# Zero matmuls ahead of the prologue, and traced costs for a planner's exponentials and score matmuls

## The chip, the cores and the metric

The kernel runs on one core of a Trainium2 chip. The metric is the device time of one execution in microseconds (us). Before the change the median of three runs is 796.83 us (796.32 to 798.67). One more execution was taken with the hardware profiler; its records are the profile and the trace read below. Five engines work at the same time, each through its own list of instructions in order: TensorE (PE, matmuls; its weight loads are shown as PEld), VectorE (DVE), ScalarE (ACT), GpSimd (POOL) and SyncE (SP), which only issues transfers here.

## The reference

Two branches are added to the input, for one sequence of 2,048 rows of 512 numbers in bf16.

```python
def _A_ref(x, wqkv, wo):                      # x: 1 x 2048 x 512, 32 heads of 16
    qkv = (x @ wqkv).reshape(B, S, 3, H, Dh).transpose(2, 0, 3, 1, 4)
    q, k, v = qkv[0], qkv[1], qkv[2]
    p = _softmax(jnp.einsum("bhqd,bhkd->bhqk", q, k) * scale, axis=-1)
    o = jnp.einsum("bhqk,bhkd->bhqd", p, v)
    return o.transpose(0, 2, 1, 3).reshape(B, S, D) @ wo

def _B_ref(x, w1, b1, w2, b2):                # F = 1376, mixes over the sequence
    u = _gelu(jnp.einsum("bsd,sf->bdf", _layernorm(x), w1) + b1)
    return (jnp.einsum("bdf,fs->bds", u, w2) + b2).transpose(0, 2, 1)

xn = _layernorm(x)
return x + _A_ref(xn, A_wqkv, A_wo) + _B_ref(xn, ...)
```

The largest piece is the softmax over 32 heads x 2,048 x 2,048 scores, 134 million exponentials.

## The kernel before

**Blocks and groups.** The scores are walked in 32 blocks (4 blocks of 512 queries, 8 groups of 4 heads), and in each block over 16 key tiles of 128 keys. A step of one key tile has two halves; each half is a score group: two matmuls of L665 (two heads of 16 in a 64-row half of the array each) into a pair of PSUM banks, 128 x 1024 numbers. Three such pairs take turns; the third (banks 4 and 5) is used for transposes and V until all 16 tiles of the input are prepared. There are 32 x 16 x 2 = 1,024 score groups.

**Two ways to exponentiate.** ScalarE does a half with one ACTIVATE (L742, `exp`). VectorE can do a key tile in its own way, a "d group": two steps of L945 (`bits`, one per half, reading a PSUM pair) and four steps over SBUF (L965, L972, L979, L985). The results go to matmuls with V (L766; four matmuls side by side are a round; a tile done by VectorE needs three rounds, one done by ScalarE needs one).

**Who decides the order.** Nothing is decided on the chip. While the kernel is built, `Dispatch` walks through a time of its own in steps of 0.01 us and gives each engine the ready step of the best priority, with costs from the table `EST`. What it chooses becomes the fixed order of each engine's list. The costs therefore change the order, and how many tiles go to VectorE (`d_ready`, L1007: only if VectorE would be free within `D_LEAD`), but not the work of an instruction. Where one instruction needs another's result on a different engine, it waits for a semaphore; the engine's later instructions stand behind it. After an exponential starts, the planner counts `exp` until ScalarE is free and `exp_lat` until its bank pair is free again; a score group costs `mm512` and is ready `pe_lat` later. `allow` (L1016) holds other matmuls back if they would make the next score late. `keep_warm` (L1070) adds pairs of matmuls with a zero matrix into the accumulating bank (L1077) where it finds TensorE short of work.

**The prologue** (L423 to L627) is written by hand in stages. GpSimd fills constants: the identity matrix, `mhalf`, `zero`, the mask `qmask`, and slots 1 to 7 of `QT`. Six loads of x go through SP and six of wqkv through ScalarE's queue. For the first four tiles VectorE takes statistics and normalises (L497, L499, L512, with an rstd on GpSimd, L501 and L503), TensorE transposes (L523), ScalarE copies the result, and TensorE makes K, Q and V of the first four heads (L536, L570, L548). At the end `qt0_evac` copies the Q of the first block: slot 0 of QT on ScalarE (L576), slot 2 on VectorE (L578), and a plain copy `qst` on ScalarE (L580), from which four transfers fill part of slots 1 and 3, which the second block reads. Two engines that read one bank do so in turn. Then the planner takes over (L629); tiles 4 to 15 are prepared beside the first exponentials (`tile_job`, L1294).

**Other work in the gaps.** The Q, K and V of further heads (L1088, L1114, L548), the second layer norm, the two large products of branch B (L1174, L1245), the output projection (L1250, L1277) and the normalisation of each block (L855 to L914) are spread over the blocks by due positions. `clear_images` has SP write zeros from QT slots 4 to 7 into a DRAM image that later Q blocks are spread through.

Of the kernel before, what the change touches and what calls it, by code (L numbers as in the profile page):

```python
# [31 lines left out]
NDB = 3  # L32
NPRE = 4
NQS = 4
NW1 = 2
# [13 lines left out]
QSCALE = 0.25 * LOG2E * 128.0  # L49
# [7 lines left out]
EST = dict(  # L57
    start=15.5, pe_switch=0.105, mm512=0.215, mm128=0.065, pe_lat=0.13,
    exp=0.924, exp_lat=1.45, tanh=0.75, act_lat=0.55,
    dve_lat=0.05, p1=1.22, ts4=0.71, tt2=1.235, cp512=0.70, cp1024=1.23, cp128=0.30,  # L60
    stats=0.92, norm=0.55, xcopy=0.43, small=0.25, stt=0.70,
# [5 lines left out]
GATE_AIM_SHORT = 6.0  # L67
D_LEAD = 0.6
S_WORK = 1.0
# [242 lines left out]
def bass_parallel_sum__softmax_full_mha__mixer_token_mlp__prompt_kernel(  # L312
# [18 lines left out]
    with ExitStack() as es:  # L331
# [19 lines left out]
        qmask = sb("qmask", [128, 2], F32)  # L351
# [3 lines left out]
        QT = sb("QT", [128, 2 * NQS, 512], BF16)  # L355
# [29 lines left out]
        zero = sb("zero", [128, 128], BF16)  # L385
# [23 lines left out]
        def bank(i):  # L409
            return ps[:, i * 512:(i + 1) * 512]  # L410
# [11 lines left out]

        sc.add("pool", lambda e: e.memset(ident[:], 0.0), writes=[("ident",)])  # L423
        sc.add("pool", lambda e: e.affine_select(ident[:], ident[:], [[-1, 128]], ALU.not_equal, 1.0,
                                                 base=0, channel_multiplier=1),
               reads=[("ident",)], writes=[("ident",)])
        sc.add("pool", lambda e: e.memset(mhalf[:], -0.5), writes=[("mhalf",)])
        sc.add("pool", lambda e: e.memset(zero[:], 0.0), writes=[("zero",)])
        sc.add("dve", lambda e: e.memset(b1c_bf[:], 0.0), writes=[("b1c",)])
# [4 lines left out]
        sc.add("dve", lambda e: e.memset(v17_main[:, :, 16:17], 1.0), writes=[("Vone",)])  # L434
        sc.add("pool", lambda e: e.memset(qmask[:], 0.0), writes=[("qmask",)])
        for r in range(4):
            sc.add("pool", lambda e, r=r: e.memset(qmask[32 * r:32 * r + 16, r % 2:r % 2 + 1], QSCALE),
                   reads=[("qmask",)], writes=[("qmask",)])
        def qt_at(b, v):
            return 4 * (b // 2 % 2) + 2 * v + b % 2  # L440

        sc.add("pool", lambda e: e.memset(QT[:, 1:2 * NQS, :], 0.0), reads=[("qmask",)],
               writes=[("QT", q) for q in range(1, 2 * NQS)])

# [130 lines left out]
        def qt0_evac():  # L575
            sc.add("act", lambda e: e.activation(QT[:, 0, :], bank(EX_BANK), ACTF.Identity, scale=qmask[:, 0:1]),  # L576
                   reads=[("bank", EX_BANK), ("qmask",)], writes=[("QT", 0)])
            sc.add("dve", lambda e: e.tensor_scalar(QT[:, 2, :], bank(EX_BANK), qmask[:, 1:2], None, ALU.mult),  # L578
                   reads=[("bank", EX_BANK), ("qmask",)], writes=[("QT", 2)])
            sc.add("act", lambda e: e.activation(qst[:, :], bank(EX_BANK), ACTF.Identity, scale=QSCALE),  # L580
                   reads=[("bank", EX_BANK)], writes=[("qst",)])
            for r in range(4):
                q = 32 * r + 16
                dma("sp", QT[q:q + 16, 1 + 2 * (r % 2), :], qst[q:q + 16, :], reads=[("qst",), ("QT", 1 + 2 * (r % 2))],
                    writes=[("QT1", r)], name="qt_spread")
# [45 lines left out]
        done = dp.done  # L631
        free_at = {("pair", 0): 0.0, ("pair", 1): 0.0, ("pair", 2): None, "b4": 0.0, "b5": 0.0, "ex": 0.0, "pv": 0.0}

# [8 lines left out]
        at[("QT", 0)] = dp.t  # L642
        at[("QT", 1)] = dp.t + 4.0

# [696 lines left out]

        def clear_job():
            def go():
                clear_images()
                dp.use("sp", 2 * EST["sp"])
            yield ("sp", 0.2, lambda: prog["p"] > 2, go)

        dp.spawn(clear_job())
        for t in range(NPRE, NT):
# [150 lines left out]
```

## Time and profile before

| what | value |
|---|---|
| median of three runs | 796.83 us |
| profiled execution, whole | 797.49 us |
| its span, first to last instruction | 795.7 us |
| mean granted clock of TensorE | 0.996 |
| ScalarE busy | 765.9 us (96%) |
| TensorE busy / VectorE busy | 723.8 us (91%) / 714.1 us (90%) |
| first exponential starts | 16.49 us |
| last exponential ends | 784.8 us |
| exponentials on ScalarE / halves on VectorE | 816 / 208 |

The page gives the busy time of each engine, the chain of work that ended last, and groups of instructions with the busy time, the mean length of one, and the idle time before them with what ended it. The timeline lists instructions in order of start: start, length, engine, line, operation, output and input, how many were merged, and in brackets the idle time before and its releaser. An instruction of ScalarE can start before the one ahead of it has ended, so the distance of starts, not the length, is what one costs.

### The profile page before, as it was taken

The page shows a single profiled execution, that of the slowest core. Times are in us where ns is not written, and L with a number is a line of the kernel's source. Part 1 is how long each engine was busy: PE and PEld are TensorE (multiplying, and loading weights), DVE is VectorE, ACT ScalarE, POOL GpSimd, SP SyncE. Part 2 cuts the span into 40 slices and gives each one's busy share as a digit, 9 for nine tenths or more (in the row PEclk, how much of TensorE's full clock was granted, in tenths as well). Part 3 has the DMA queues.
Part 4 walks back from the last instruction along what each step waited for, and adds up shares of the span by engine and source line. Part 5 has one row for each costly group of instructions (what it writes and reads, how often), then busy time and mean ns, then how long its engine had stood idle before and what let it go on. Part 6 is the DMA issues. An engine that isn't in the chain of part 4 may idle for free.

```text
span 795.7 us, 14239 instructions
## 1 busy us (share of the span) xinstructions
PE 723.8 (91%) x5928; PEld 212.0 (27%) x5928; DVE 714.1 (90%) x948; ACT 765.9 (96%) x838; POOL 73.0 (9%) x110
## 2 busy tenths in 40 slices
PE   5999998999999899999899989999999999989885
PEld 3433332322222222222222222222222222222221
DVE  6888988999999799999999989998999999998888
ACT  4999999999999999999999999999999999999994
POOL 5233000000000010000000000000000000000000
PEclk9999999999999999999999999999999999999998
DMA  7402010102112122120302212112131112111001
GB/s 187 110 12 70 16 51 15 38 15 74 45 41 67 39 50 68 41 57 15 96 20 56 72 35 79 36 35 79 42 96 33 50 47 82 45 48 49 16 5 40
DMA packets 85184, 41.28 MB, mean 52 GB/s; under 512 B 61184, under 2 KB 81152, under 8 KB 85120
## 3 DMA queue, kind: packets, MB, share of 16 engines
q1 hardware_dynamic: 81952, 38.80, 18.3%
q10 hardware_dynamic: 3168, 1.57, 0.7%
q8 instruction: 46, 0.75, 0.4%
q14 instruction: 18, 0.15, 0.1%
HBM read 33.69 MB, written 5.37 MB: 49 GB/s over the span
## 4 chain that ended last, share of the span: by engine, by line
ACT 71%; PE 17%; DVE 9%; DMA 1%; issue 1%; POOL 0%; SPq 0%; ACTq 0%; DVEq 0%
ACT pT L742 71%; PE ps L665 7%; PE ps L766 5%; DVE xreg L945 3%; DVE big L979 1%; PE ps L1245 1%; PE ps L1174 1%; DMA xreg<-in_A_x_dram 1%; PE ps L1088 1%; DVE xreg L985 1%; DVE stats L497 0%; PE ps L1077 0%; DVE denb L1435 0%; DVE dmore L972 0%; ACT ga_sb L1203 0%
## 5 line engine op out<-in xcount | busy, mean ns | idle before, releaser
L742 ACT ACTIVATE pT<-ps 128x1024 bf16<-128x1024 f32 x816 | 756.5, 1131 | 8.2 <-PE ps L665 5.9
L665 PE MATMUL ps<-QT,KT 64*128 64x512 bf16 x2048 | 361.1, 385 | 52.7 <-ACT pT L742 30.7
L945 DVE TENSOR_SCALAR xreg<-ps 128x1024 int16<-128x1024 f32 x208 | 254.4, 1223 | 58.0 <-PE ps L665 53.6
L665 PEld LDWEIGHTS ps<-QT,KT 64*128 64x128 bf16 x2048 | 88.8, 93 | 338.9 <-ACT pT L742 219.8
L766 PE MATMUL ps<-pT,V 128*32 128x512 bf16 x1632 | 152.6, 388 | 1.2 <-ACT pT L742 0.9
L979 DVE TENSOR_TENSOR big<-xreg,big 128x2048 bf16<-128x2048 bf16 x104 | 128.2, 1233 | 0.0
L985 DVE TENSOR_SCALAR xreg<-xreg 128x2048 int16<-128x2048 int16 x104 | 73.2, 703 | 1.6
L965 DVE TENSOR_SCALAR big<-xreg 128x2048 int16<-128x2048 int16 x104 | 71.0, 683 | 0.1
L766 PEld LDWEIGHTS ps<-pT,V 128*32 128x32 bf16 x1632 | 37.6, 94 | 91.3 <-issue 84.6
L1245 PE MATMUL ps<-gT,w2blk 128*128 128x512 bf16 (+1 forms) x176 | 54.5, 385 | 0.0
L1174 PE MATMUL ps<-big,w1blk 128*128 128x512 bf16 (+1 forms) x176 | 52.9, 385 | 0.0
L895 POOL TENSOR_TENSOR oTe<-OT,denb 128x512 bf16<-128x512 f32 x15 | 20.7, 1380 | 337.6 <-DVE big L979 107.9
L766 PE MATMUL ps<-big,V 128*32 128x512 bf16 x556 | 48.2, 380 | 0.1
L766 PE MATMUL ps<-xreg,VS 128*32 128x512 bf16 x416 | 40.4, 379 | 0.2 <-DVE xreg L985 0.2
L895 POOL TENSOR_TENSOR oT<-OT,denb 128x512 bf16<-128x512 f32 x12 | 15.9, 1326 | 240.0 <-DMA denb<-den_scr 140.9
L972 DVE TENSOR_SCALAR xreg<-xreg 128x2048 int16<-128x2048 int16 x35 | 25.4, 725 | 0.0
L548 PE MATMUL ps<-wqkv_sb,xnT 128*128 128x128 bf16 x256 | 24.4, 225 | 0.1
L972 DVE TENSOR_SCALAR dmore<-xreg 128x2048 int16<-128x2048 int16 x34 | 24.4, 718 | 0.0
L972 DVE TENSOR_SCALAR big<-xreg 128x2048 int16<-128x2048 int16 x35 | 23.9, 683 | 0.0
L1077 PE MATMUL ps<-xnT,zero 128*128 128x512 bf16 x72 | 21.4, 384 | 0.4 <-ACT KT L518 0.2
L855 DVE COPY OT<-ps 128x512 f32<-128x512 f32 x31 | 21.2, 683 | 0.3 <-PE ps L766 0.2
L503 POOL TENSOR_TENSOR mv<-mv,mhalf 128x1 f32<-128x1 f32 x32 | 18.8, 586 | 2.7
(79 smaller groups left out, 373.0 us busy)
## 6 DMA issues: line engine op xcount, KB each, us to landing
denb<-den_scr SPq DMA_DIRECT2D x31, 256.0 KB
QT<-q_img SPq DMA_DIRECT2D x15, 512.0 KB
w1blk<-in_B_w_dram SPq DMA_DIRECT2D x10, 512.0 KB
w2blk<-in_B_w_dram SPq DMA_DIRECT2D x16, 320.0 KB
w1blk<-in_A_x_dram SPq DMA_DIRECT2D x16, 128.0 KB
out_dram<-osb SPq DMA_DIRECT2D x16, 128.0 KB, 1.7
q_img<-qst SPq DMA_DIRECT2D x30, 64.0 KB
xreg<-in_A_x_dram SPq DMA_DIRECT2D x3, 512.0 KB, 9.1
```

The source lines that it names most:

```text
L548: sc.add("pe", lambda e, ct=ct: e.matmul(bank(bk)[:, 128 * j:128 * (j + 1)], lhsT=xnT[:, ct, 128 * t:128 * (t + 1)], rhs=wqkv_sb[:, ct, 2 ...
L665: sc.add("pe", lambda e: e.matmul(bank(bk), lhsT=KT[64 * (r // 2):64 * (r // 2) + 64, T, 128 * kt:128 * (kt + 1)], rhs=QT[64 * (r // 2):64 ...
L742: sc.add("act", lambda e: e.activation(pT[:, buf, :], ps[:, s_ * 1024:(s_ + 1) * 1024], ACTF.Exp, scale=EXP_SCALE), reads=[("bank", 2 * s_ ...
L766: sc.add("pe", lambda e, r=r, lhs=lhs, rhs=rhs: e.matmul(bank(PV_BANK)[32 * r:32 * r + 32, :], lhsT=lhs, rhs=rhs, start=first, stop=last, ...
L895: sc.add("pool", lambda e: e.tensor_tensor(dst, OT32[:, eb, :], denb[:, :], ALU.mult), reads=[("OT32", eb), ("denb",)], writes=keys, extra ...
L945: sc.add("dve", lambda e: e.tensor_scalar(bv_i[:, i, 1024 * hf:1024 * (hf + 1)], ps[:, s_ * 1024:(s_ + 1) * 1024], EXP_BIAS, 0.0, ALU.add, ...
L965: sc.add("dve", lambda e: e.tensor_scalar(ge_i[:, i, :], bv_i[:, i, :], 0x7F, 0x3F00, ALU.bitwise_and, ALU.bitwise_or), reads=[("bD", i)], ...
L972: sc.add("dve", lambda e: e.tensor_scalar(vp_i(i), bv_i[:, i, :], 0x7F80, None, ALU.bitwise_and), reads=[("bD", i)], writes=[("vD", i)] + ...
L979: sc.add("dve", lambda e: e.tensor_tensor(ge_f[:, i, :], bv_f[:, i, :], ge_f[:, i, :], ALU.mult), reads=[("bD", i), ("eD", i)], writes=[(" ...
L985: sc.add("dve", lambda e: e.tensor_scalar(bv_i[:, i, :], bv_i[:, i, :], LIN_S, None, ALU.add), reads=[("bD", i)], writes=[("bD", i)])
L1174: mms = [lambda st=st: sc.add("pe", lambda e: e.matmul(bank(EX_BANK)[0:m, :], lhsT=w1blk[:, slot, st, 0:m], rhs=h_sb[:, st, :], start=(st ...
L1245: mms.append(lambda ft=ft, m=m: sc.add("pe", lambda e: e.matmul(bank(EX_BANK), lhsT=w2blk[0:m, slot, ft, :], rhs=gT[0:m, ft, :], start=(ft ...
```

## The change

A tile of zeros is cleared first, and nine matmuls with it go into bank 4 ahead of everything on TensorE. The clears of `qmask` move from GpSimd to VectorE. The one large clear of QT slots 1 to 7 on GpSimd becomes six clears of one slot each, given out by the planner (slot 2 is written whole and gets none). The copy to `qst` and its four transfers leave the prologue and become a planned job behind the third exponential's scores; the clear of the images may be issued sooner. In the table, `start`, `exp`, `exp_lat`, `pe_lat` and `dve_lat` get new values, and `D_LEAD` goes from 0.6 to 1.0. In the built order `qst` stands behind two exponentials, ScalarE has 822 exponentials and VectorE 202 halves, and the L1077 kind has 60 matmuls instead of 72.

```diff
+NWARM = 9
...
-    start=15.5, pe_switch=0.105, mm512=0.215, mm128=0.065, pe_lat=0.13,
-    exp=0.924, exp_lat=1.45, tanh=0.75, act_lat=0.55,
-    dve_lat=0.05, p1=1.22, ts4=0.71, tt2=1.235, cp512=0.70, cp1024=1.23, cp128=0.30,
+    start=12.0, pe_switch=0.105, mm512=0.215, mm128=0.065, pe_lat=0.215,
+    exp=0.90, exp_lat=1.13, tanh=0.75, act_lat=0.55,
+    dve_lat=0.0, p1=1.22, ts4=0.71, tt2=1.235, cp512=0.70, cp1024=1.23, cp128=0.30,
...
-D_LEAD = 0.6
+D_LEAD = 1.0
...
-        sc.add("pool", lambda e: e.memset(ident[:], 0.0), writes=[("ident",)])
+        sc.add("pool", lambda e: e.memset(zero[:], 0.0), writes=[("zero",)])
+        for _ in range(NWARM):
+            sc.add("pe", lambda e: e.matmul(
+                bank(4), lhsT=zero[:, :], rhs=zero[:, :].unsqueeze(1).broadcast_to([128, 4, 128]), start=True, stop=True),
+                reads=[("zero",)], writes=[("bank", 4)])
+        sc.add("pool", lambda e: e.memset(ident[:], 0.0), reads=[("zero",)], writes=[("ident",)])
...
-        sc.add("pool", lambda e: e.memset(zero[:], 0.0), writes=[("zero",)])
...
-        sc.add("pool", lambda e: e.memset(qmask[:], 0.0), writes=[("qmask",)])
+        sc.add("dve", lambda e: e.memset(qmask[:], 0.0), writes=[("qmask",)])
         for r in range(4):
-            sc.add("pool", lambda e, r=r: e.memset(qmask[32 * r:32 * r + 16, r % 2:r % 2 + 1], QSCALE),
+            sc.add("dve", lambda e, r=r: e.memset(qmask[32 * r:32 * r + 16, r % 2:r % 2 + 1], QSCALE),
...
-        sc.add("pool", lambda e: e.memset(QT[:, 1:2 * NQS, :], 0.0), reads=[("qmask",)],
-               writes=[("QT", q) for q in range(1, 2 * NQS)])
+        def clear_qt(q):
+            sc.add("pool", lambda e: e.memset(QT[:, q, :], 0.0), writes=[("QT", q)])
...
+        def qst0():
             sc.add("act", lambda e: e.activation(qst[:, :], bank(EX_BANK), ACTF.Identity, scale=QSCALE),
                    reads=[("bank", EX_BANK)], writes=[("qst",)])
+
+        def qst0_spread():
             for r in range(4):
...
-        free_at = {("pair", 0): 0.0, ("pair", 1): 0.0, ("pair", 2): None, "b4": 0.0, "b5": 0.0, "ex": 0.0, "pv": 0.0}
+        free_at = {("pair", 0): 0.0, ("pair", 1): 0.0, ("pair", 2): None, "b4": 0.0, "b5": 0.0, "ex": None, "pv": 0.0}
...
         def clear_job():
+            for k, q in enumerate((1, 3, 4, 5, 6, 7)):
+                def go(q=q):
+                    clear_qt(q)
+                    dp.use("pool", 0.5)
+                    if q == 3:
+                        at[("QT13",)] = dp.t + 0.6
+                yield ("pool", 0.6, lambda k=k: prog["p"] > 0.5 + 0.5 * k, go)
...
-            yield ("sp", 0.2, lambda: prog["p"] > 2, go)
-
+            yield ("sp", 0.2, lambda: True, go)
+
+        def qst0_job():
+            def go():
+                qst0()
+                free_at["ex"] = dp.use("act", 0.6) + 0.2
+                at[("qst0",)] = free_at["ex"]
+            yield ("act", 0.0, lambda: a_cur["n"] > 2, go)
+
+            def go():
+                qst0_spread()
+                at[("QT", 1)] = dp.use("sp", 4 * EST["sp"]) + EST["dma"]
+            yield ("sp", 0.1, lambda: done(("qst0",), ("QT13",)), go)
```

More of the change, by code (lines that the diff above doesn't have):

```diff
@@ L642, in bass_parallel_sum__softmax_full_mha__mixer_token_mlp__prompt_kernel @@
         at[("QT", 0)] = dp.t
-        at[("QT", 1)] = dp.t + 4.0
         def blk_of(b):
@@ L1345, in go @@
                 dp.use("sp", 2 * EST["sp"])
-            yield ("sp", 0.2, lambda: prog["p"] > 2, go)
+            yield ("sp", 0.2, lambda: True, go)
[9 more added lines that the diff above has]
+            yield ("sp", 0.1, lambda: done(("qst0",), ("QT13",)), go)
+        dp.spawn(qst0_job())
         dp.spawn(clear_job())
```

## The prediction

> **What bounds the kernel now.** I read the page's busy times and chain of waits first, then ScalarE's timeline from start to end, then the timeline of the first 20 us on the other engines.
>
> ```profile
> PE 723.8 (91%) x5928; PEld 212.0 (27%) x5928; DVE 714.1 (90%) x948; ACT 765.9 (96%) x838; POOL 73.0 (9%) x110
> ...
> ACT 71%; PE 17%; DVE 9%; DMA 1%; issue 1%; POOL 0%; SPq 0%; ACTq 0%; DVEq 0%
> ...
> L742 ACT ACTIVATE pT<-ps 128x1024 bf16<-128x1024 f32 x816 | 756.5, 1131 | 8.2 <-PE ps L665 5.9
> L665 PE MATMUL ps<-QT,KT 64*128 64x512 bf16 x2048 | 361.1, 385 | 52.7 <-ACT pT L742 30.7
> L945 DVE TENSOR_SCALAR xreg<-ps 128x1024 int16<-128x1024 f32 x208 | 254.4, 1223 | 58.0 <-PE ps L665 53.6
> ```
>
> ScalarE sets the end: 96% busy, 71% of the chain, nearly all in the 816 exponentials of L742. The other 208 of the 1,024 halves of score groups are done by VectorE (L945), which waits 58.0 us for scores and is not the bound. So the span is: first exponential, plus their number times their distance, plus what they wait, plus the tail.
>
> ```profile
> 14.26 0.69 ACT L576 ACTIVATE QT<-ps,qmask 128x512 bf16<-128x512 f32 x1 [0.25 <-PE ps L570]
> 15.84 0.60 ACT L580 ACTIVATE qst<-ps 128x512 bf16<-128x512 f32 x1 [0.90 <-DVE QT L578]
> 16.33 0.27 ACT L518 ACTIVATE KT<-ps 128x128 bf16<-128x128 f32 x1
> 16.49 11.37 ACT L742 ACTIVATE pT<-ps 128x1024 bf16<-128x1024 f32 x12
> ...
> 32.57 1.94 ACT L742 ACTIVATE pT<-ps 128x1024 bf16<-128x1024 f32 x2 [0.29 <-PE ps L665]
> 34.80 68.00 ACT L742 ACTIVATE pT<-ps 128x1024 bf16<-128x1024 f32 x74 [0.29 <-PE ps L665]
> ...
> 702.14 82.65 ACT L742 ACTIVATE pT<-ps 128x1024 bf16<-128x1024 f32 x90 [0.17 <-PE ps L665]
> ```
>
> The columns are start, length, engine, line. Between neighbouring exponentials the starts lie 0.904 us apart in the median and never under 0.903, but 0.934 in the mean: about 24 us of waiting in all, of which only the 8.2 of the groups' row shows as idle, since an exponential's 1.13 us overlaps the next. The sum closes: 16.49 + 816 x 0.904 (737.7) + 11 tanh at 0.52 (188.73 to 189.25 in ScalarE's timeline; 5.7) + 24 = 783.9, against an end of the exponentials at 702.14 + 82.65 = 784.8. The tail from there to the span's 795.7 is 10.9.
>
> **Part 1, the first exponential.** L580 stands ahead of it and waits for VectorE's L578, since two engines read one bank in turn. The first score pair was ready: it starts at 15.00, and a score's second matmul stands at least 0.43 ahead of its exponential (least distance in the trace), so 15.45 was possible. Moving L580 behind two exponentials gives 1.04. It still costs 0.49 (15.84 to 16.33) later in the stream, but there it falls into a pause: after the second score come six zero matmuls (L1077, 1.47 long) before the third.
>
> Zero matmuls: nine of 128x512. Four cold 128-column matmuls step by 0.43 in the rows below, so nine 512-column ones take 9 x 0.43 = 3.9 us, while TensorE has nothing else until 6.78. What a faster clock gains is bounded by VectorE:
>
> ```profile
> 9.05 0.69 DVE L497 BATCH_NORM_STATS2 stats<-xreg 128x6 f32<-128x512 bf16 x1
> 12.34 0.41 DVE L512 TENSOR_SCALAR big<-xreg,mv 128x512 bf16<-128x512 bf16 x1
> 12.87 0.29 DVE L519 CAST KT<-ps 128x128 bf16<-128x128 f32 x1
> ```
> ```profile
> 13.05 0.63 PE L548 MATMUL ps<-wqkv_sb,xnT 128*128 128x128 bf16 x4
> 13.48 0.51 PE L536 MATMUL ps<-xnT,wqkv_sb 128*128 128x128 bf16 x4
> 13.83 0.39 PE L570 MATMUL ps<-xnT,wqkv_sb 128*128 128x128 bf16 x4
> ```
>
> The 9.05 start follows the landing of x tiles 4 to 7 at 9.03 (2.12 + 6.91 in the chain), and the change moves no load. From there VectorE's order is unchanged up to KT of tile 2. That copy can come at 12.34 + 0.38 = 12.7 instead of 12.87; it frees the bank, so the last tile's L536 and L570 start at 13.03 and 13.25 instead of 13.48 and 13.83. QT then starts 0.58 earlier. The faster chain that GpSimd's shortened opening allows (its 3.09 us clear of QT, 2.34 to 5.43, delays the first statistics) ends in that same wait for 9.03, so it is worth nothing; likewise the five qmask clears on VectorE (0.54 us on GpSimd for four) are covered, by up to 0.8 us. Without the cover they would cost 0.6. With both effects the first exponential starts at 14.9 instead of 16.49. The third: second QT 0.75 after the first, score at 15.25, zero matmuls 15.5 to 16.9, then exponential at 17.35, against 18.49. Gain there 1.1, the postponed L580 included.
>
> The Trainium skill ("TensorE: Matmul & The Clock Gate", Part 1) says that the clock opens after some 3.4 us of sustained activity in a free-running window. The rows agree: 0.63 per group up to 13.05, 0.39 from 13.83, after TensorE ran almost unbroken since 10.52. By that rule nine matmuls are just enough, or not, by the window's phase.
>
> If the clock stays cold, 1.04 is left of the first gain and about 0.5 at the third exponential. That lower end I keep.
>
> **Part 2, the tiles.** Up to 34.80 tiles 4 to 15 pass through VectorE at 2.23 us each (28.11, 30.34, 32.57, 34.80), and 18 exponentials that need 16.3 us take 18.3: 2.0 lost. In the new order the statistics of tiles 14 and 15 (each 0.68 + 0.18 + 0.38) stand behind the tile that the 19th exponential needs, no longer before it. That moves 2.5 us of VectorE away and clears most of the 2.0; I take 1.3 (bounds 0 and 2.0). Against it stand six clears of QT, 3.09 / 7 = 0.44 each, 2.6 us on GpSimd, four of them in a row between two rstd steps. In the old trace GpSimd idles 2.40 us before 22.00, which covers that row of 1.8; if cover fails, the next norm is late by up to 1.8. I take 0.3.
>
> ```profile
> 781.50 1.95 POOL L895 TENSOR_TENSOR oT<-OT,denb 128x512 bf16<-128x512 f32 x1 [26.05 <-DMA denb<-den_scr]
> ...
> 782.35 1.64 DVE L985 TENSOR_SCALAR xreg<-xreg 128x2048 int16<-128x2048 int16 x1
> ```
>
> Here a VectorE step of 0.70 (its mean) took 1.64 beside GpSimd's work. The skill's page "SBUF — State Buffer", section "SBUF: two separate sides", calls it an exclusive lock for some pairs of instructions, and so speaks against moving clears from the idle opening into the stage that VectorE sets. By it all 2.6 us could be lost; by the old clear, beside which L497 ran its usual 0.69 twice, nothing.
>
> Start in all: -1.1 - 1.3 + 0.3 = -2.1, bounds -3.5 and +1.0. SP's queue keeps its order (spread of qst, clears of the images, w1 loads); the spread block is first read by the 33rd exponential, at 47.5 us in the trace, against about 24 for its landing, so moving it costs nothing.
>
> **Part 3, the division.** With exp at 0.90 and D_LEAD at 1.0 the built order gives ScalarE 822 exponentials and VectorE 202 (three groups fewer). Six more at 0.904 are +5.4. VectorE saves 3 x (2 x 1.22 + 1.23 + 3 x 0.70) = 17.3 us, which is worth nothing, since it does not set the end. The twelve zero matmuls (60 of L1077's form instead of 72) and twelve fewer rounds of L766 free TensorE, also beside the path.
>
> **Part 4, the waits.** They come from the order, so I sort the exponentials after the first 26 by what freed their two banks, in both built orders, and price each class by the old trace (22.7 us there). Tight: freed by the exponential two places before. 320 of these lost 17.0 us, 53 ns each; there are now 385. Freed by VectorE: 139 lost 5.4, 39 ns; now 107. Freed three or more places before: 1 ns. Sum 20.4 + 4.1 + 0.3 = 24.8, +2.1. Sorted further by the TensorE work (in 0.22 us slots) between two scores: tight with two slots 63 ns, 129 before and 122 now; with four or more 238 ns, 31 before and 35 now; VectorE-freed with four, 349 ns, 8 before and 2 now. That sum is 21.9, -0.8; by slots of two neighbouring gaps it is 27.8, +5.1. I take +0.5; the ends are +5.1 and -16 (if the traced estimates place work so well that every tight one loses the 5 ns of those with at most one slot).
>
> **Tail.** After VectorE's last scores 15 exponentials remain (10 before), 13.6 us, over a chain of some 9 us on VectorE; the last steps are the same. Zero; if VectorE were late, up to 0.7 per step.
>
> Sum: -2.1 + 5.4 + 0.5 = +3.8. The profiled execution took 797.49, so 801.3; the median of the runs, 796.83, lies 0.66 lower, so 800.6.
>
> **Rivals.** (a) Waits shrink: the old estimates put an exponential's release at 1.45, the trace has the dependent score from 1.06; work held by the true value loses less. For it: 14 of the 22.7 us sit in tight ones with two or four slots. Against: those classes are as numerous as before. If half of it goes (7.6), 793.0. This ends on the other side, and decides from about 6.2 us saved, where 2.4 below the old median is reached. (b) The start gains its full 3.5 and the waits fall by 1.5: 796.83 - 3.5 + 5.4 - 1.5 = 797.2. For it: 18.3 us lie between the first and the 19th exponential where 16.3 would do; against: the clears. (c) Two-gap prices, and tight exponentials now prevail because VectorE's scores are issued up to 1.0 us early and hold a pair: 800.6 + 4.6 = 805.2. (d) The zero matmuls do not open the clock in time, so that part does nothing: 801.2.
>
> **How the numbers follow.** The forecast has 0.50 (own range 798 to 803), (a) 0.22, (b) 0.13, (c) 0.11, (d) 0.04. About 0.3%, 2.4 us, is what a measurement here can tell from no change: limits 794.4 and 799.2. Faster: 0.17 of (a) and 0.03 of (b), 0.20. Slower: 0.42 of the forecast, 0.02 of (b), (c) and (d), 0.59. Same: 0.21. The range 792.0 to 806.0 leaves out the far parts of (a) and (c).
>
> **What would show it.** Right: first exponential at 14.9, the run that began at 34.80 with the 19th now reached some 2 us earlier, 822 exponentials at 0.904, L665-caused waits of 22 to 25 us in all, tail near 11. Wrong: mean distance of exponentials at 0.92 or less (rival a), a first exponential before 14, VectorE steps of twice their length beside the clears, or a clock below full in the middle of the span.

## The result and the profile after

The changed kernel takes 798.54 us (median of 15 runs, 797.60 to 799.59); the kernel before took 796.42 us beside it (15 runs, 795.25 to 798.67). The ratio of the runs is 1.0022, interval 1.0014 to 1.0030: 1.75 us slower (the two medians lie 2.12 apart), about half of the +3.8 that the prediction's sum gave. One profiled execution among the experiments below, that of old_release, ran at a mean granted clock of 0.939 and took 802.8 us against its kernel's median of 800.54; nothing is concluded from its waits alone.

First the page of the changed kernel: busy times, the engines' shares of the chain that ended last, and the three costliest groups.

```profile
PE 714.2 (90%) x5813; PEld 215.0 (27%) x5901; DVE 699.6 (88%) x935; ACT 769.4 (97%) x844; POOL 71.4 (9%) x110
...
ACT 81%; PE 13%; DVE 4%; DMA 1%; issue 1%; POOL 0%; SPq 0%; ACTq 0%; DVEq 0%
...
L750 ACT ACTIVATE pT<-ps 128x1024 bf16<-128x1024 f32 x822 | 759.7, 1125 | 6.2 <-PE ps L673 3.4
L673 PE MATMUL ps<-QT,KT 64*128 64x512 bf16 x2048 | 362.7, 384 | 56.0 <-ACT pT L750 41.6
L953 DVE TENSOR_SCALAR xreg<-ps 128x1024 int16<-128x1024 f32 x202 | 247.0, 1223 | 65.6 <-PE ps L673 63.5
```

ScalarE still sets the end, more plainly than before: 81% of the chain instead of 71%, 822 exponentials instead of 816. VectorE does six halves fewer and waits 65.6 us for scores instead of 58.0; that idle time costs nothing. What ScalarE waits ahead of an exponential fell from 8.2 to 6.2 us. Then ScalarE's timeline (start, length, engine, line):

```profile
13.97 0.69 ACT L581 ACTIVATE QT<-ps,qmask 128x512 bf16<-128x512 f32 x1 [0.19 <-PE ps L575]
14.55 0.27 ACT L523 ACTIVATE KT<-ps 128x128 bf16<-128x128 f32 x1
15.14 2.08 ACT L750 ACTIVATE pT<-ps 128x1024 bf16<-128x1024 f32 x2 [0.32 <-PE ps L673]
17.12 0.59 ACT L587 ACTIVATE qst<-ps 128x512 bf16<-128x512 f32 x1
17.93 3.81 ACT L750 ACTIVATE pT<-ps 128x1024 bf16<-128x1024 f32 x4 [0.22 <-PE ps L673]
22.09 86.27 ACT L750 ACTIVATE pT<-ps 128x1024 bf16<-128x1024 f32 x94 [0.36 <-PE ps L673]
...
647.02 138.03 ACT L750 ACTIVATE pT<-ps 128x1024 bf16<-128x1024 f32 x150 [0.49 <-PE ps L673]
```

The copy qst now stands behind two exponentials, and the short runs of the tile stage are gone: from 22.09 on 94 exponentials follow each other, where before the run of 74 began at 34.80. The end of the exponentials is 647.02 + 138.03 = 785.05.

The two profiled executions split as the prediction's sum does. "Waits" is what the starts of the exponentials lie apart over 0.904 us each.

| us | before | after | difference |
|---|---|---|---|
| first exponential | 16.49 | 15.14 | -1.35 |
| waits up to the 27th | 2.11 | 1.66 | -0.45 |
| (start of the 27th) | 42.10 | 40.31 | -1.79 |
| exponentials x 0.904 | 816 | 822 | +5.42 |
| waits from there to the last, 11 tanh included | 27.99 | 24.73 | -3.26 |
| tail after the last exponential | 10.89 | 10.88 | 0.0 |
| span | 795.67 | 795.93 | +0.26 |

(The last exponential itself was 0.1 shorter.) The spans of the profiles differ by 0.26 and the timed runs by 1.75 to 2.12 because the profiled execution of before was 1.1 us above its median and that of after 0.7 below. Where the 1.1 lies is seen further down: in the waits. The start of the first exponential also differs from execution to execution of one opening: 15.14 is the earliest of twelve profiles of the new opening with its zero matmuls (up to 16.75, mean 15.91), while seven of the old opening have 16.49 to 17.22, mean 16.83. So the -1.35 of this pair is 0.9 in the mean.

### The profile page after: what moved, and what is told of

Read it like the earlier page. It is cut to its first block, busy times and chain, and to the rows that moved or that the text cites. A ratio compares the mean times of both kernels' runs of the same rounds, so it can differ in the third digit from the quotient of the medians.

```text
span 795.9 us, 14106 instructions
## 1 busy us (share of the span) xinstructions
PE 714.2 (90%) x5813; PEld 215.0 (27%) x5901; DVE 699.6 (88%) x935; ACT 769.4 (97%) x844; POOL 71.4 (9%) x110
## 4 chain that ended last, share of the span: by engine, by line
ACT 81%; PE 13%; DVE 4%; DMA 1%; issue 1%; POOL 0%; SPq 0%; ACTq 0%; DVEq 0%
ACT pT L750 80%; PE ps L673 5%; PE ps L774 4%; PE ps L1182 2%; DVE xreg L953 1%; DMA xreg<-in_A_x_dram 1%; DVE big L987 1%; PE ps L1253 1%; ACT ga_sb L1211 1%; DVE denb L1464 0%; PE ps L1096 0%; DVE osb L1454 0%; DVE big L973 0%; POOL mv L508 0%; PE ps L541 0%
## 5 line engine op out<-in xcount | busy, mean ns | idle before, releaser
L953 DVE TENSOR_SCALAR xreg<-ps 128x1024 int16<-128x1024 f32 x202 | 247.0, 1223 | 65.6 <-PE ps L673 63.5
L673 PEld LDWEIGHTS ps<-QT,KT 64*128 64x128 bf16 x2048 | 90.5, 93 | 340.3 <-ACT pT L750 264.0
L774 PE MATMUL ps<-pT,V 128*32 128x512 bf16 x1644 | 157.0, 389 | 1.7 <-ACT pT L750 1.4
L987 DVE TENSOR_TENSOR big<-xreg,big 128x2048 bf16<-128x2048 bf16 x101 | 126.6, 1254 | 0.0
L993 DVE TENSOR_SCALAR xreg<-xreg 128x2048 int16<-128x2048 int16 x101 | 70.1, 694 | 1.3
L774 PEld LDWEIGHTS ps<-pT,V 128*32 128x32 bf16 x1644 | 39.5, 93 | 100.5 <-issue 91.9
L1253 PE MATMUL ps<-gT,w2blk 128*128 128x512 bf16 (+1 forms) x150 | 48.6, 384 | 4.0 <-issue 4.0
L1182 PE MATMUL ps<-big,w1blk 128*128 128x512 bf16 (+1 forms) x155 | 48.2, 385 | 3.3 <-issue 3.3
L903 POOL TENSOR_TENSOR oTe<-OT,denb 128x512 bf16<-128x512 f32 x15 | 19.8, 1322 | 322.0 <-DMA denb<-den_scr 96.2
L980 DVE TENSOR_SCALAR xreg<-xreg 128x2048 int16<-128x2048 int16 x34 | 23.2, 683 | 0.0
L980 DVE TENSOR_SCALAR dmore<-xreg 128x2048 int16<-128x2048 int16 x33 | 22.6, 684 | 0.0
L863 DVE COPY OT<-ps 128x512 f32<-128x512 f32 x31 | 21.2, 683 | 0.9 <-PE ps L774 0.7
L508 POOL TENSOR_TENSOR mv<-mv,mhalf 128x1 f32<-128x1 f32 x32 | 18.5, 577 | 2.7
L553 PEld LDWEIGHTS ps<-wqkv_sb,xnT 128*128 128x128 bf16 x256 | 15.5, 99 | 9.5 <-issue 8.8
```

Of the source, the lines that this page charges most:

```text
L553: sc.add("pe", lambda e, ct=ct: e.matmul(bank(bk)[:, 128 * j:128 * (j + 1)], lhsT=xnT[:, ct, 128 * t:128 * (t + 1)], rhs=wqkv_sb[:, ct, 2 ...
L673: sc.add("pe", lambda e: e.matmul(bank(bk), lhsT=KT[64 * (r // 2):64 * (r // 2) + 64, T, 128 * kt:128 * (kt + 1)], rhs=QT[64 * (r // 2):64 ...
L774: sc.add("pe", lambda e, r=r, lhs=lhs, rhs=rhs: e.matmul(bank(PV_BANK)[32 * r:32 * r + 32, :], lhsT=lhs, rhs=rhs, start=first, stop=last, ...
L903: sc.add("pool", lambda e: e.tensor_tensor(dst, OT32[:, eb, :], denb[:, :], ALU.mult), reads=[("OT32", eb), ("denb",)], writes=keys, extra ...
L953: sc.add("dve", lambda e: e.tensor_scalar(bv_i[:, i, 1024 * hf:1024 * (hf + 1)], ps[:, s_ * 1024:(s_ + 1) * 1024], EXP_BIAS, 0.0, ALU.add, ...
L980: sc.add("dve", lambda e: e.tensor_scalar(vp_i(i), bv_i[:, i, :], 0x7F80, None, ALU.bitwise_and), reads=[("bD", i)], writes=[("vD", i)] + ...
```

## The experiments

Each kernel was timed beside the kernel before on the same chip; ratios stand with their 95% intervals, and a ratio difference of 0.001 is 0.8 us. "Waits" are from here on those between neighbouring exponentials after the 27th (before 22.2 us, after 19.0; tanh left out), which the profile of each kernel gives.

**The prologue and the estimates apart.** prologue_alone is the changed kernel with the old table of estimates and D_LEAD 0.6; estimates_alone is the kernel before with the new ones (start left at 15.5):

```
-    start=15.5, ... pe_lat=0.13,        +    start=15.5, ... pe_lat=0.215,
-    exp=0.924, exp_lat=1.45, ...        +    exp=0.90, exp_lat=1.13, ...
-    dve_lat=0.05, ...                   +    dve_lat=0.0, ...
-D_LEAD = 0.6                            +D_LEAD = 1.0
```

> The changed prologue (zero matmuls, six clears, the later qst) with all old estimates and D_LEAD 0.6: 816 exponentials, and behind the tiles the built order is that of the kernel before. Theory A, start and later waits are separate terms: first exponential at 15.1 us, the 27th at 40.3 to 41.0 instead of 42.1, waits between neighbouring exponentials after the 27th unchanged at 22.2 us, time 1.1 to 1.8 us under the kernel before (ratio 0.9977 to 0.9986). Rival B, the gain among the tiles comes from the new estimates' order: the first at 15.1, but the 27th within 0.5 of 42.1, ratio 0.9994 or more.

Measured 797.67 us, 1.0011 (1.0000 to 1.0022). Theory A falls: the first exponential came at 15.83, but the waits up to the 27th rose from 2.11 to 3.59 us, and the 27th began at 42.92. B's ratio holds; its 27th, within 0.5 of 42.1, does not.

> The old prologue with the new estimates and D_LEAD 1.0: 822 exponentials, and behind the tiles the built order is that of the changed kernel. Theory A, the new order waits less: first exponential at 16.5, waits after the 27th about 19.0 us as in the changed kernel instead of 22.2, time 5.4 - 3.3 = 2.1 to 3.5 us over the kernel before (ratio 1.0026 to 1.0044). Rival B, the smaller waits of the one profiled execution of the changed kernel were chance or came from its earlier start: waits 22 us, 5.4 us over (ratio 1.0068).

Measured 799.69 us, 1.0035 (1.0024 to 1.0045). Theory A holds: the ratio lies in its range, and the waits are 19.3. So the prologue gains 1.0 us beside the new estimates (1.0035 to 1.0022, with overlapping intervals) and loses 0.9 beside the old ones. The estimates also cut the tile stage's losses: up to the 27th exponential 1.49 us are waited in estimates_alone, 2.11 before.

**The move of qst.** From the start of QT's copy on ScalarE to the first exponential it is 2.23 us in all seven profiles of the old opening (14.26 to 16.49 before) and 1.17 to 1.39 in the thirteen of the new one (13.97 to 15.14 in the changed kernel): about 1.06 gained, where the forecast had 1.04. But the third exponential starts 2.79 us after the first instead of 2.00. ScalarE now waits 0.97 us on both sides of the second exponential, where it waited 0.20, so most of that gain is paid back two exponentials later.

**The zero matmuls**, taken out by NWARM = 0:

> The changed kernel without the nine zero matmuls, all else in the same order. Theory A, they open the clock a little sooner: QT of the first block 0.3 us later, first exponential at 15.4 instead of 15.1, time 0.3 us over the changed kernel (ratio to the kernel before 1.0026). Rival B, the 0.58 us that the prediction gave to a clock open from the first tile: 0.6 us over. Rival C, they do nothing: same time as the changed kernel, 1.0022.

Measured 798.63 us, 1.0018 (1.0009 to 1.0028), the same as with them: C. First VectorE's timeline of the changed kernel (its third and fifth statistics):

```profile
6.70 0.69 DVE L502 BATCH_NORM_STATS2 stats<-xreg 128x6 f32<-128x512 bf16 x1 [0.83 <-DMA xreg<-in_A_x_dram]
...
9.15 0.69 DVE L502 BATCH_NORM_STATS2 stats<-xreg 128x6 f32<-128x512 bf16 x1
```

The third statistics waits 0.83 us for x tiles 2 and 3. They landed at 6.67 here, at 5.92 in the profile of before, and at 7.29, 7.48 and 7.86 in those of estimates_alone, prologue_alone and no_zero; no edit touches that load. In the new prologue VectorE waits for it each time, 0.83, 1.63 (prologue_alone) and 2.02 us (no_zero), and here then for tiles 4 to 7, which land at 9.12. The fifth statistics starts at 9.44 in the mean of the seven profiles of the old opening and at 9.57 in the thirteen of the new: so the shorter chain on GpSimd brings nothing forward.

A faster clock of TensorE does. From the fifth statistics to QT's copy it is 4.66 and 4.67 us in the two profiles whose granted clock was full from 12.0 and 12.2 us on (estimates_alone, after_lat115), and 5.53 and 5.52 in the two where it became full for good only at 15.6 and 19.8, behind that copy (dve_mid, old_exp). But the zero matmuls do not decide when: that stretch takes 5.20 in the mean of the twelve profiles with them and 5.15 in the seven of the old opening. What they do to the clock stands in the last section.

**The six clears of QT.** pro_clear_early is prologue_alone with the one large clear back ahead of the tiles:

```
-        def clear_qt(q):
-            sc.add("pool", lambda e: e.memset(QT[:, q, :], 0.0), writes=[("QT", q)])
+        sc.add("pool", lambda e: e.memset(QT[:, 1:2 * NQS, :], 0.0),
+               writes=[("QT", q) for q in range(1, 2 * NQS)])
```

> The changed prologue with all old estimates and D_LEAD 0.6, but with QT cleared by GpSimd in one instruction ahead of the tiles, as before, instead of six between them: 816 exponentials. Theory A (the six clears delay the norms and rstd steps of the tiles, where VectorE sets the pace): the norms beside them take 0.41 us again, the 27th exponential starts 0.5 to 0.9 us earlier than the 42.9 of the kernel with the clears, ratio 1.000 to 1.0006. Theory B (the clears cost nothing, and the late tile stage comes from the landing of the x loads): the 27th exponential at 42.5 or later, ratio 1.001 as with the clears.

Measured 797.14 us, 1.0000 (0.9991 to 1.0009). Theory A holds by the waits up to the 27th exponential, which fall from 3.59 to 2.91 us, and by the ratio, which falls by 0.0011, though the two intervals overlap. The 27th started at 42.59, 0.33 earlier only and so on B's side of its bound, since the first exponential was 0.35 later in this execution. prologue_alone, GpSimd's clears and VectorE's norm beside them:

```profile
20.36 2.06 POOL L448 MEMSET QT<- 128x512 bf16 x4
...
20.44 0.58 DVE L517 TENSOR_SCALAR big<-xreg,mv 128x512 bf16<-128x512 bf16 x1 [0.46 <-POOL mv L508]
```

pro_clear_early, the same norm:

```profile
20.26 0.41 DVE L517 TENSOR_SCALAR big<-xreg,mv 128x512 bf16<-128x512 bf16 x1 [0.15 <-POOL mv L508]
```

The norm takes 0.58 instead of 0.41 and starts after 0.46 of idle time instead of 0.15. The norm's idle time is GpSimd's: its rstd step (L508) stands behind a clear. In the changed kernel the same norm takes 0.58 after 0.46, and the wait of 0.48 us ahead of the seventh exponential (22.09 in the timeline above) is 0.03 in pro_clear_early. So there the clears cost 0.45.

**One estimate at a time.** old_exp is the changed kernel with exp=0.924; old_release has exp_lat=1.45 and pe_lat=0.13; old_lead10 is the kernel before with D_LEAD = 1.0 alone; old_rel_lead10 is old_lead10 with exp_lat=1.13 and pe_lat=0.215.

> The changed kernel with exp back at 0.924, all else as changed: 818 exponentials, 373 tight, 106 freed by VectorE. Theory A, exp only moves the division: waits 19 to 21 us, time 3.6 us less 0 to 2 for waits: 1.6 to 3.6 us under the changed kernel (ratio to the kernel before 0.9977 to 1.0002). Rival B, an exponential believed longer than it is leaves ScalarE dry: waits 24 us or more, at least 1.4 us over the changed kernel (1.004).

Measured 797.82 us, 1.0016 (1.0007 to 1.0025), 818 exponentials, waits 22.1: between the two theories. 2.2 us of waiting fell between the second and the third exponential, 0.8 in the changed kernel.

> The changed kernel with the two estimates of release and readiness back at their old values (exp_lat 1.45, pe_lat 0.13), exp and D_LEAD as changed: 818 exponentials, 307 tight and 149 freed by VectorE after the 27th. Theory A, the traced release estimates are what shortened the waits: 22 us or more between neighbours after the 27th, 3.6 us gained by four exponentials fewer and 3 lost, same time as the changed kernel within 1 us (ratio to the kernel before 1.001 to 1.003). Rival B, the estimates of release do little and the prices of the changed kernel's classes hold: waits 15 us, 7.6 us under the changed kernel (ratio 0.993).

Measured 800.54 us, 1.0051 (1.0038 to 1.0064), 818 exponentials: theory A's direction, and further. Four exponentials fewer are -3.6, and yet it is 2.3 us over the changed kernel.

> The kernel before with D_LEAD alone at 1.0 and nothing else changed: 814 exponentials instead of 816. Theory A (the shorter waits after VectorE's scores come from the traced release times of ScalarE and TensorE; the larger lead only changes the division): the prices per class stay those of before, 53 ns for a tight one and 39 ns for one freed by VectorE. With 357 and 118 of them that is 18.9 + 4.6 = 23.5 us against 22.2, so +1.3 and two exponentials less, -1.8: ratio 0.999 to 1.000. Theory B (the larger lead, which issues VectorE's scores earlier, is what shortens the waits): the prices are those of the changed kernel, 48 and 10 ns, 17.1 + 1.2 = 18.3 us, so -3.9 - 1.8 = -5.7: ratio 0.993. The number to read is the mean wait of an exponential freed by VectorE: 39 ns by A, 10 ns by B.

Measured 795.63 us, 0.9976 (0.9968 to 0.9985), waits 21.1; an exponential freed by VectorE waited 27 ns. Between the two theories, and nearer to A: two exponentials fewer are -1.8 of the -1.9.

> The kernel before with the traced release times exp_lat 1.13 and pe_lat 0.215 and D_LEAD 1.0; exp 0.924, prologue and start as before. 816 exponentials, as before; 373 tight and 111 freed by VectorE, nearly the counts of the changed kernel. Theory A (the traced releases shorten the waits): like the three orders of the changed kernel, 17.9 to 22.6 us and 19.9 in the mean, 2.3 under before: ratio 0.997, between 0.9945 and 1.0005. Theory B (the two groups are one, the order decides): as around the kernel before, 20.5 to 23.9 us or more, ratio 0.998 to 1.002 or above. Below 0.998 speaks for A, above 1.000 for B.

Measured 803.72 us, 1.0088 (1.0072 to 1.0103), waits 28.1. Theory A falls. In this order the traced release times do not shorten the waits; with exp at 0.924 they came with the longest but one of all. Its waits on ScalarE (total, times, longest):

```profile
ACT pT L742 <- PE ps L766: 7.1, 4, 3.0
ACT pT L742 <- PE ps L665: 6.5, 19, 0.5
```

About half of this idle time are four waits that PV matmuls end (L766), where before has one of 1.3. That kind is the subject of the next pair.

**The lead.** lead06 is the changed kernel with D_LEAD = 0.6 (826 exponentials); lead06_npb12 is lead06 with NPB = 12 instead of 10 (828).

> The changed kernel with D_LEAD back at 0.6: 826 exponentials on ScalarE, 326 tight ones after the 27th (375 in the changed kernel), 146 freed by VectorE (107). Theory A, D_LEAD is what makes VectorE's scores early and so shortens waits behind it: the 146 cost 39 ns each as before the change, the tight ones 48, waits 21 to 22 us; with four more exponentials 3.6 + 2.5 = 6 us over the changed kernel (ratio to the kernel before 1.010). Rival B, D_LEAD only makes more tight exponentials: waits 326 x 48 + 146 x 10 ns = 17 us, 3.6 - 2 = 1.6 us over the changed kernel (1.0042).

Measured 809.78 us, 1.0157 (1.0137 to 1.0176), more than either theory gave. Against the changed kernel, four exponentials are +3.6 and the waits, 26.1 instead of 19.0, +7.1. First its waits on ScalarE, then one of them in the timeline of all engines:

```profile
ACT pT L750 <- PE ps L774: 10.0, 5, 3.0
ACT pT L750 <- PE ps L673: 2.5, 9, 0.5
```
```profile
280.06 1.23 DVE L953 TENSOR_SCALAR xreg<-ps 128x1024 int16<-128x1024 f32 x1 [0.33 <-PE ps L673]
281.20 0.68 DVE L863 COPY OT<-ps 128x512 f32<-128x512 f32 x1
...
281.94 1.26 PE L774 MATMUL ps<-pT,V 128*32 128x512 bf16 x20 [0.20 <-DVE OT L863]
282.61 1.94 ACT L750 ACTIVATE pT<-ps 128x1024 bf16<-128x1024 f32 x2 [3.03 <-PE ps L774]
```

At the end of a block the PV matmuls of the next block need the bank that VectorE copies out (L863). VectorE was still at a score until about 281.2, so the copy came late, twenty PV matmuls had piled up, and ScalarE stood for 3.03 us until they had run. That it stood for want of a free pT buffer is tested next.

> The changed kernel with D_LEAD 0.6 and twelve buffers of pT instead of ten: 828 exponentials (826 with ten). Theory A (with the small lead the exponentials run out of pT buffers at the ends of blocks, while PV matmuls wait for VectorE's copy of the accumulating bank): two more buffers hold 1.8 us more of ScalarE's work, so the waits of L750 that PV matmuls end fall from 10.0 us to 3 or less, and the time lies 5 us or more under the 809.8 with ten buffers: ratio 1.010 or less. Theory B (those waits come from the order itself, since the larger division makes VectorE's share end late whatever the buffers): the waits move to other enders, the time stays at 808 to 812: ratio 1.015 to 1.019.

Measured 806.88 us, 1.0114 (1.0096 to 1.0131). With twelve buffers no wait that PV matmuls end is left in the list; it begins:

```profile
ACT pT L750 <- PE ps L673: 5.5, 14, 0.8
```

Waits fall to 21.2. The mechanism of theory A holds; its time does not in full (2.9 us less instead of 5), since the new order has two more exponentials (+1.8) and its waits for scores rose from 2.5 to 5.5.

**Neighbouring orders.** Five kernels move one constant so little that the classes hardly change: after_lat115 and after_lat111 (the changed kernel, exp_lat 1.15 and 1.11 instead of 1.13), after_exp902 (exp 0.902), before_lead059 (the kernel before, D_LEAD 0.59), before_lat147 (exp_lat 1.47 instead of 1.45).

> The changed kernel with exp_lat 1.15 instead of 1.13: 822 exponentials as there, another order in places (375 tight and 107 freed by VectorE, as there, but other TensorE work between the scores). Theory A (the traced estimates make the waits short): 19 us between neighbours after the 27th exponential, within 1 us, and ratio 1.002 within 0.001. Theory B (each order has its own waits, whatever its class counts): the waits differ from 19.0 by 2 us or more, and the ratio by as much: 0.999 or less, or 1.005 or more.

Measured 797.63 us, 1.0010 (1.0001 to 1.0020), waits 17.9: A.

> The changed kernel with exp_lat 1.11 instead of 1.13: 822 exponentials as there, 359 tight and 113 freed by VectorE. Theory A (the traced estimates make the waits short): at the prices of the changed kernel, 48 and 10 ns, 17.2 + 1.1 = 18.3 us, so ratio 1.001 to 1.002. Theory B (each order has its own waits): they differ from 18.3 by 2 us or more, and the ratio with them: 0.999 or less, or 1.004 or more.

Measured 802.39 us, 1.0072 (1.0056 to 1.0088), waits 22.6: B. A change of 0.02 us in one estimate, with the same 822 exponentials, costs 4.0 us, about twice what the whole change costs. One of its long waits, in the timeline of all engines:

```profile
600.22 1.27 POOL L903 TENSOR_TENSOR big<-OT,denb 128x512 bf16<-128x512 f32 x1 [26.17 <-DMA denb<-den_scr]
...
601.62 0.75 DVE L1268 SCALAR_TENSOR_TENSOR big<-ps,b2col,w1blk 128x512 f32<-128x512 f32 x1 [1.92 <-POOL big L903]
...
602.29 1.22 DVE L953 TENSOR_SCALAR xreg<-ps 128x1024 int16<-128x1024 f32 x1
...
603.56 0.39 PE L673 MATMUL ps<-QT,KT 64*128 64x512 bf16 x2 [1.46 <-DVE xreg L953]
...
604.65 1.02 ACT L750 ACTIVATE pT<-ps 128x1024 bf16<-128x1024 f32 x1 [1.16 <-PE ps L673]
```

Read it from the top: GpSimd's step waited for a DMA; VectorE's L1268 stood 1.92 us behind GpSimd; the score half queued behind it on VectorE (L953) came late; TensorE could not refill that pair for 1.46 us; and ScalarE idled 1.16. No count of bank pairs tells of this.

> The kernel before with D_LEAD 0.59 instead of 0.6: 816 exponentials as there, 303 tight and 143 freed by VectorE. Theory A (the waits belong to the old estimates): at the prices of before, 53 and 39 ns, 16.1 + 5.6 = 21.7 us, against 22.2: ratio 0.999 to 1.000. Theory B (each order has its own waits): they differ by 2 us or more, so ratio 0.997 or less, or 1.0025 or more.

Measured 796.73 us, 0.9994 (0.9983 to 1.0004), waits 20.5: A in the time.

> The kernel before with exp_lat 1.47 instead of 1.45: 816 exponentials as there, 313 tight and 136 freed by VectorE. Theory A (the waits belong to the old estimates): at the prices of before, 16.6 + 5.3 = 21.9 us, ratio 0.999 to 1.001. Theory B (each order has its own waits): they differ by 2 us or more, so ratio 0.9975 or less, or 1.0025 or more.

Measured 799.65 us, 1.0036 (1.0023 to 1.0049), waits 23.9: B in the time. Its one wait that PV matmuls end is 2.3 us long, against 1.3 before.

> The changed kernel with exp 0.902 instead of 0.90: 820 exponentials, two fewer, -1.8 us; 366 tight and 108 freed by VectorE. Theory A (the traced estimates keep the waits near 19): at 48 and 10 ns 17.6 + 1.1 = 18.7 us, so ratio 0.999 to 1.000. Theory B (each order has its own waits): anywhere from 17.9 to 22.6 as in the three orders run so far, so ratio 0.9985 to 1.0045; 1.002 or more, with the two exponentials less, speaks for B.

Measured 798.05 us, 1.0020 (1.0010 to 1.0029), waits 20.8; by its stated bound of 1.002 it speaks for B, if barely.

**VectorE's estimates.** The table left p1, ts4, tt2 and cp512 at 1.22, 0.71, 1.235 and 0.70. dve_traced sets them to 1.14, 0.60, 1.20 and 0.61 (810 exponentials), dve_mid to 1.18, 0.66, 1.22 and 0.66 (814); old_dve_mid10 puts those of dve_mid and D_LEAD 1.0 into the kernel before (806).

> The changed kernel with VectorE's estimates also set to the distances that the trace shows (p1 1.14, ts4 0.60, tt2 1.20, cp512 0.61): 810 exponentials on ScalarE, 214 halves on VectorE, 375 tight ones, 103 freed by VectorE. Theory A, the number of exponentials sets the time: 12 fewer at 0.904 are 10.8 us, waits by class 20 us instead of 19: 9.7 us under the changed kernel (ratio to the kernel before 0.990). Rival B, VectorE's spare time is what lets it copy the finished block's bank in time: long waits of 1 to 3 us behind the matmuls with V at block ends, 7 us more of waits, 3 us under the changed kernel (0.9985).

Measured 792.87 us, 0.9949 (0.9938 to 0.9961), waits 23.8: between the two, 5.8 us under the changed kernel.

> The changed kernel with VectorE's estimates half way to the traced ones (p1 1.18, ts4 0.66, tt2 1.22, cp512 0.66): 814 exponentials, 378 tight, 109 freed by VectorE. Theory A: 8 fewer exponentials are 7.2 us, waits as in the changed kernel: 7.2 us under it (ratio to the kernel before 0.993). Rival B, waits at block ends grow by 3 to 4 us: 3.5 us under it (0.998).

Measured 792.87 us, 0.9952 (0.9940 to 0.9964), waits 20.2: between the two again, 5.6 under the changed kernel. Both are about 4 us under the kernel before: with estimates too long only for VectorE, the dispatcher gives ScalarE, which sets the end, more than its share.

> The kernel before with VectorE's four estimates half way to their traced values and D_LEAD 1.0, all else as before: 806 exponentials, ten fewer, -9.0 us. Theory A (the waits follow the classes at the prices of before): 317 tight ones at 53 ns and 152 freed by VectorE at 39 ns are 22.7 us against 22.2, so -8.5: ratio 0.989. Theory B (fewer exponentials are partly paid back, because VectorE then becomes late, as in the changed kernel where four exponentials instead of twelve fewer came with 3.2 us less in waits): waits rise by 4 to 6, so -3 to -5: ratio 0.994 to 0.996.

Measured 794.82 us, 0.9969 (0.9957 to 0.9981), waits 28.3: B's direction, and just past its far end.

**Does the count explain the times?** Executions of one order differ too: prologue_alone and pro_clear_early have the order of before behind their opening, and their waits were 20.6 and 20.2 against its 22.2 (mean 21.0); no_zero and estimates_alone have the order of the changed kernel, 19.0 and 19.3 against 19.0 (mean 19.1). With these means, "number x 0.904 plus waits", the ones up to the 27th included, against the parent kernel:

| kernel (parent) | exponentials | waits up to / after the 27th | worked out, us | measured, us |
|---|---|---|---|---|
| before | 816 | 2.1 / 21.0 | | |
| before_lead059 | 816 | 2.1 / 20.5 | -0.5 | -0.5 |
| before_lat147 | 816 | 2.1 / 23.9 | +2.9 | +2.9 |
| old_lead10 | 814 | 2.1 / 21.1 | -1.7 | -1.9 |
| old_rel_lead10 | 816 | 1.6 / 28.1 | +6.6 | +7.0 |
| old_dve_mid10 | 806 | 2.1 / 28.3 | -1.7 | -2.5 |
| changed kernel | 822 | 1.7 / 19.1 | | |
| after_lat115 | 822 | 1.7 / 17.9 | -1.2 | -1.0 |
| after_lat111 | 822 | 1.7 / 22.6 | +3.5 | +4.0 |
| after_exp902 | 820 | 1.7 / 20.8 | -0.1 | -0.2 |
| old_exp | 818 | 3.0 / 22.1 | +0.7 | -0.5 |
| lead06 | 826 | 1.7 / 26.1 | +10.6 | +10.8 |
| lead06_npb12 | 828 | 1.7 / 21.2 | +7.5 | +7.3 |
| dve_mid | 814 | 1.6 / 20.2 | -6.2 | -5.6 |
| dve_traced | 810 | 1.7 / 23.8 | -6.1 | -5.8 |

Measured is the difference of the two ratios times 796.4. But for old_exp, whose profiled execution was 1.6 us above its median, they agree within 0.8, most within 0.4. For a profiled execution such a sum is true by its making; what the table tests is whether one profile of a kernel speaks for its timed runs, and it does. So the accounting stands: a plan is worth its number of exponentials and its own waits. The number is read from the built order without running it; the waits were not.

## Why the prediction was wrong

**Failed: Part 4, the waits, "I take +0.5".** The waits fell. The profiles give -3.26 from the 27th exponential on; with the means over the executions of each order it is 19.1 - 21.0 = -1.9, which agrees with what the medians leave: +1.75 = start -1.6, division +5.4, rest -2.0. The prediction priced each class by the trace of before, "53 ns" for 385 tight ones and "39 ns" for 107 freed by VectorE, 24.5 us. Its counts were near (375 and 107 between neighbours, beside tanh left out), its prices were not: 48 ns and 10 ns, 18.9 us. Over the executions of each order the tight ones cost 18.0 us instead of 16.2 (20.4 by the prediction's price) and those freed by VectorE 1.1 instead of 4.5 (4.1 by its price).

The runs show that such a price is no property of a class. after_lat115 has the same 375 tight ones at 44 ns; in old_rel_lead10 373 of them cost 68 ns; the VectorE-freed cost 10 to 78 ns over these orders. Part of the difference are long waits: those of over 0.35 us, 13 to 28 in an order and up to 3.4 us long, sum to 7.7 us in the changed kernel, 10.5 in after_lat111 and 17.5 in old_rel_lead10. These steps of 2.8 and 9.8 stand against 3.6 and 9.1 by which all waits differ. In old_dve_mid10, with 28.3 in all, the long ones are only 12.1 and none is over 0.74, so there it is many short ones. The two looked at, at the end of a block and behind a late DMA, are of a kind that a sort by bank pairs does not see.

Whether a part of the -1.9 belongs to the traced estimates as such stays open. The four orders of the changed kernel average 20.1 (19.1, 17.9, 22.6, 20.8) and the four around before 21.6 (21.0, 20.5, 23.9, 21.1): a shift of 1.5, less than the spread of 4.7 and 3.4 within the groups.

**Part 3, the division: right in its +5.4,** 822 exponentials at 0.904. VectorE's busy time fell by 14.5 us. That this is worth nothing is not shown: the exponentials freed by VectorE waited 3.4 us less, though in lead06, where VectorE has still less to do, they waited 6.1 in all. The rounds of L766 are six fewer, not twelve (2,856 matmuls instead of 2,880).

**Parts 1 and 2, the start: near in sum, not in its terms.** Forecast -2.1 at the end of the tiles; the profiles give -1.79, the timed runs about -1.6 (prologue -1.0, the tile order -0.6). Part 1 was to have gained 1.1 at the third exponential. In this pair of profiles it is 0.56 (17.93 instead of 18.49), and with the mean first exponential of each opening about 0.1. Moving qst gave its 1.06 at the first and then took back 0.8, where the forecast had about 0.5. The 0.58 that the zero matmuls were to add at QT is the size of what an early clock gives, but they did not give it: the prediction asked whether nine are enough to open the clock, and took for nothing that it closes again before the work arrives. So the doubt of rival (d) held. The first exponential came at 15.14 instead of 14.9 by the luck of one execution. From the third exponential to the 27th, Part 2 forecast -1.0 (-1.3 for the order, +0.3 for the clears), and the profiles give -1.23; the clears cost 0.45 there, and 0.7 in the old order. That bears out in part what the prediction drew from the Trainium skill ("SBUF — State Buffer", section "SBUF: two separate sides"): one norm took 0.58 instead of 0.41, but four clears in a row did not lock VectorE out for their 2.06 us.

**Tail: right,** 10.88 against 10.89.

**Rivals.** (a) had the right sign, but its reason does not hold in every order: the true release times were to save by themselves, and in old_rel_lead10 they added 7.0 us of waits to old_lead10's 21.1, while in old_release the old ones cost time. (b) took the waits at -1.5 and the start at -3.5; the first was near, the second was not. (c) falls: the waits went down, not up.

## What to carry to other kernels

Where one engine sets the end and a planner places its work, price a change of the planner's estimates by the count that it gives that engine, which the built order tells exactly, and treat the waits as a draw with a spread: here 3 to 5 us of 796 between orders that differ by 0.002 to 0.02 us in one estimate. Before crediting an estimate with a small gain, run two or three neighbours of it. And correct the estimates of all engines that share the work together: tracing those of ScalarE and TensorE alone moved work onto the engine that was already the bound.

## What the runs showed of the hardware

**A GpSimd step beside VectorE depends on when a DMA lands.** Before, VectorE's and GpSimd's timeline, with TensorE's score behind them:

```profile
456.31 1.27 POOL L895 TENSOR_TENSOR big<-OT,denb 128x512 bf16<-128x512 f32 x1 [24.34 <-DMA denb<-den_scr]
456.34 1.79 DVE L972 TENSOR_SCALAR dmore<-xreg 128x2048 int16<-128x2048 int16 x1
...
459.32 0.39 PE L665 MATMUL ps<-QT,KT 64*128 64x512 bf16 x2 [1.24 <-DVE xreg L945]
```

prologue_alone, the same place of the same order:

```profile
456.81 0.68 DVE L980 TENSOR_SCALAR dmore<-xreg 128x2048 int16<-128x2048 int16 x1
...
457.62 1.27 POOL L903 TENSOR_TENSOR big<-OT,denb 128x512 bf16<-128x512 f32 x1 [25.17 <-DMA denb<-den_scr]
...
458.55 1.42 DVE L987 TENSOR_TENSOR big<-xreg,big 128x2048 bf16<-128x2048 bf16 x1
```

Where GpSimd's step began 0.03 us ahead of VectorE's, that one took 1.79 us instead of 0.68, and the next exponential came 0.96 us late; where the DMA landed later, the step lay beside another instruction (L987, 1.42 instead of the 1.21 of L979 at that place before), and no exponential came late. The Trainium skill ("SBUF — State Buffer", section "SBUF: two separate sides") calls it an exclusive lock held for the whole instruction. The row nearly agrees: fully blocked, L972 would have taken 1.27 - 0.03 + 0.68 = 1.92. Before, 11 VectorE instructions beside one of the 31 such steps take over 0.1 us longer than the median of their kind, 7.5 us in all; in the other profiles it is 8 to 17 of them and 4.7 to 9.7 us. That is one source of the 1.6 to 2.0 us by which executions of one order differed.

**The clock opened and closed again.** TensorE's timeline of lead06, the zero matmuls and the first two groups of four transposes:

```profile
1.00 3.54 PE L426 MATMUL ps<-zero 128*128 128x512 bf16 x9 [1.00 <-POOL zero L424]
5.92 0.40 PE L528 MATMUL ps<-ident,big 128*128 128x128 bf16 x4 [1.39 <-DVE big L517]
7.76 0.61 PE L528 MATMUL ps<-ident,big 128*128 128x128 bf16 x4 [1.44 <-DVE big L517]
...
13.72 0.59 PE L541 MATMUL ps<-xnT,wqkv_sb 128*128 128x128 bf16 x4
14.15 0.39 PE L575 MATMUL ps<-xnT,wqkv_sb 128*128 128x128 bf16 x4
```

Here the zero matmuls did open the clock (0.40 for four transposes), it was lost again behind the pauses (0.61), and it came back at 14.15. In the changed kernel's profile the transposes at 5.92 took 0.61 at once. The granted clock in the traces tells the same. In seven of the twelve profiles with zero matmuls it was full, or 0.95 in old_release, from 3.9 to 5.4 us on, each time for 3.41 us, then half for 3.41 or 6.83 us, and back only at 12.2 to 15.6. In those first 3.41 us TensorE was busy for 0.4 to 1.2 us, with pauses of up to 2.4. In the other five it was full first at 13.0 to 19.8, no earlier than in the eight profiles without them (12.0 to 15.5). So in this prologue they opened the clock in some executions, and the work behind them kept it in none.
